# Another hand-written order for the head of a retention and two-GLU kernel

## The chip, the core and the metric

One core of one Trainium2 chip runs the whole program. The metric is device microseconds (us) of one execution, lower is better. The kernel before takes 632.54 us (median of 3 runs, 631.24 to 632.9).

## The reference, cut to what matters

A retention layer (linear attention with a decay for each of 8 heads) over 2 sequences of 768 tokens feeds a GLU (1536 tokens, 512 to 1536 to 512), whose output feeds a normalised SwiGLU of the same size.

```python
for t in range(S):                       # retention; gamma depends on the head
    state = gamma * state + k_t (outer) v_t
    y_t   = scale * q_t @ state
x = y.reshape(1536, 512)
x = ((x @ w_a) * (x @ w_b)) @ w_out      # first GLU
xn = x / sqrt(mean(x * x) + 1e-6) * rms_g
out = (silu(xn @ w_gate) * (xn @ w_val)) @ w_out2
```

## The kernel before, in words

The retention is computed in 12 chunks n = 0 to 11 of 128 tokens; chunk n belongs to sequence n mod 2, so chunk n needs the state that chunk n - 2 left. The GLUs work in f32r with every operand split into a high and a low part (three TensorE passes for a product). Weights come from HBM as 64-bit numbers and are converted on ScalarE and VectorE.

Nothing is scheduled at run time: each engine and each DMA queue executes its instructions in the order in which the Python code issues them, and an instruction whose operand is not ready holds up all behind it on its engine. For the head, that is the retention and the first four products of the first GLU, this order is the string HEAD: a list of tokens, a letter and a number, each looked up in the table `does` and called in turn. After the head a planner places the rest of the two GLUs; its clocks are set equal when the head is over.

What the tokens issue, with their engine:

- `lw`, `lq`, `lk`, `L`, `m`, `d`: loads by the SP queue. `lw` is the next weight tile (`raw`), `lq n` the q and k of the scores of chunk n, `lk n` its k and v, `L n` both, `m` the mask, `d` the query decay `dq_sb` (256 KB; all the others 512 KB). The tiles of `lq` have three buffers, so a fourth load of this kind waits until the scores have read the first.
- `warm n`: n TensorE products of a tile of zeros, whose result is not used.
- `S n` (`scores`): 8 TensorE products q times k into two banks `sc`, then two VectorE products with the mask, `p` (one for each bank).
- `W n`, `w n` (`prep_v`): v times its decay, `vd`, on VectorE or on GpSimd. `Q n`, `q n` (`prep_q`): q times its decay, `qd`, on GpSimd or on VectorE. `D c`: the decay of a later pair of chunks on ScalarE.
- `T n` (`state`): 8 TensorE products `vd` times k into the state `st`, all states in one bank, then a ScalarE copy of it, `sd`, for chunk n + 2. The next T waits for that copy.
- `P n` (`past`): 8 TensorE products of `sd` and `qd` (nothing for chunks 0 and 1). `V n` (`values`): 8 TensorE products of `p` and v into the same banks `ya`; ScalarE rounds them to `xh`, VectorE makes the rest `xl`. `F n`: a ScalarE copy `xf`.
- `c`, `x`: `c` begins the conversion of the next weight tile, `x` issues the next step of each conversion under way (ScalarE `u` and `v`; VectorE a shift, a bit merge, an addition; ScalarE `uh`; VectorE `ul`).
- `Ua i`, `Ub i` (`half`): the two halves, 12 TensorE products of 512 columns each, of product i of the first GLU. `G`, `R`: gate and split of its result. `t`: a step of the tasks that follow.

The lines of the profile name the helper that issues (L87 for VectorE, ScalarE and GpSimd, L96 for TensorE), so work is told apart by its tiles.

Of the kernel before, what the change touches and what calls it, by code (L numbers as in the profile page):

```python
# [11 lines left out]
AF = mybir.ActivationFunctionType  # L12
# [3 lines left out]
B, H, S, D = 2, 8, 768, 64  # L16
P = 128
# [23 lines left out]


FIRST = (0, 0), (0, 1), (1, 0), (1, 1)
HEAD = "lw lq0 m lk0 L1 lq2 d warm15 c0 lk2 x x S0 lq3 lw lk3 warm5 W0 x x P0 V0 F0 x w1 Q2 x T0 S1 L4 lw lw P1 T1 V1 F1 S2 P2 V2 S3 F2 Q3 w2 c0 x W3 P3 x V3 F3 T2 x D2 S4 x L5 L6 Q4 W4 Ua0 L7 T3 x c1 x Q5 W5 x Ub0 G0 x R0 S5 T4 P4 V4 F4 x L8 D3 Q6 W6 x S6 T5 P5 V5 F5 c1 L9 Q7 W7 x S7 x T6 P6 V6 x L10 D4 F6 W8 x P7 Q8 V7 S8 T7 x L11 F7 q9 W9 x t0 x t1 c1 x Ua1 x Ub1 G1 x S9 T8 P8 V8 x R1 D5 Q10 x t1 c1 x Ua2 x x Ub2 G2 x S10 P9 V9 x Q11 x t1 R2 x T9 Ua3 x x x Ub3 G3 x S11 T10 P10 V10 x t1 R3 P11 V11"
UP = {"P1": (1, 0), "P2": (5, 1), "P6": (4, 2), "P7": (3, 3), "P5": (2, 4), "P3": (7, 5), "P4": (6, 6)}


# [20 lines left out]
def retention_glu_swiglu(ctx: ExitStack, tc: tile.TileContext, qk, kv, dq, mask, dg, eye, w1, w2, rg, out):  # L68
# [22 lines left out]
    vec, act, gps = Engine(nc.vector, "vec", 70, 1.04), Engine(nc.scalar, "act", 100, 0.83), Engine(nc.gpsimd, "gps", 120, 2.2)  # L91
# [12 lines left out]
    def mult(o, a, b, engine=vec):  # L104
        engine.tensor_tensor(o, a, b, op=ALU.mult)
# [9 lines left out]
    scale = cst.tile([P, LINE // 4], F32R, name="scale")[:, :2 * NB * TPB].rearrange("p (w j t) -> p w j t", j=NB, t=TPB)  # L115
# [9 lines left out]
    def bank(tag, name):  # L125
        if tag in rings:
            rings[tag].append(rings[tag].pop(0))
            tag = rings[tag][-1]
        return ps.tile([P, TB], F32, tag=tag, name=name)
# [11 lines left out]
    def load_w():  # L141
        if n_load[0] < len(kinds):
            f, s = kinds[n_load[0]]
            t = cp.tile([P, DM, 2], I32, tag="raw", bufs=3, name=f"raw{f}_{s}")
            src = (w1 if f < NF else w2)[f % NF, :, s, :].bitcast(I32)
            nc.sync.dma_start(t.rearrange("p n t -> p (n t)"), src)
            raws[f, s] = t
            n_load[0] += 1
# [94 lines left out]
    class Task:  # L243
# [3 lines left out]
        def step(self):  # L247

            was, after_pe[0], ends[0] = after_pe[0], self.ready, 0.0
            got = next(self.g, "done")  # L250
            after_pe[0] = was
            self.ready = max(self.ready, ends[0])
            if got == "done":
                tasks.remove(self)
            elif got in work:
                self.on = got
            return got != "wait"
# [94 lines left out]
    def rest(ffn, f, j, h, engine=vec):  # L352
        hh, hl = hs[ffn, f, j]
        sub(hl, h, hh.bitcast(F32), engine=engine)
        h_ready.add((ffn, f, j))
# [206 lines left out]
    with tc.manual_schedule():  # L562

        xf = {}
        with ExitStack() as att:
# [7 lines left out]
            dk_sb = dg_sb[:, :CPB * H].rearrange("p (c h) -> p c h", h=H)  # L573
            gq_sb = dg_sb[:, CPB * H:CPB * (H + NP)].rearrange("p (c n) -> p c n", n=NP)
            st = bank("S", "st").rearrange("p (b n d) -> p b n d", b=B, n=NP)
            qk_t, kv_t = {}, {}
# [13 lines left out]
            qd_t, vd_t, sd_t, p_t, ya_t, y_t, dq_t = {}, {}, {}, {}, {}, {}, {1: dq_sb}  # L590
# [6 lines left out]
            def prep_q(n, engine=gps):  # L597
                if n >= B:
                    qd_t[n] = ap.tile([P, NP, C], F32, tag="qd", bufs=QD, name=f"qd{n}")
                    mult(qd_t[n], qk_t[n][:, 0], dq_t[n // B], engine=engine)  # L600

            def prep_v(n, engine=vec):
                c = n // B
                if c < CPB - 1:
                    vd_t[n] = ap.tile([P, H, D], F32, tag="vd", name=f"vd{n}")
                    mult(vd_t[n], kv_t[n][:, 1], dk_sb[:, c, :, None].to_broadcast([P, H, D]), engine=engine)

            def scores(n):
                p_t[n] = a2.tile([P, 2, NP, C], F32, tag="p", name=f"p{n}")
# [76 lines left out]
            def half(i, r):  # L686
                f, j = FIRST[i]
                if r == 0:
                    g_t[i] = one.tile([P, TB], F32, tag=f"g{n_unit[0] % 2}", name=f"g{n_unit[0]}")
                    n_unit[0] += 1  # L690
                b = bank("A", f"c{f}_{j}_{r}")
                passes = [(2 * k + e, w[:, o, e * P:(e + 1) * P], x) for k, o in enumerate(((1, 5), (0, 6))[r]) for e in range(2)
                          for w, x in zip((ups[f][0], ups[f][0], ups[f][1]), (xs[0, j][y] for y in (0, 1, 0)))]
                if f == r == 0:
                    passes.sort(key=lambda p: p[2] is xs[0, j][1])
                for n, (k, w, x) in enumerate(passes):
                    mm(b, w, x[:, k, :], start=(n == 0), stop=(n == len(passes) - 1))
                if r == 0:
                    act.copy(g_t[i], b)
                else:  # L700
                    g_t[i, 1] = b
                    jobs(0, f, j)
# [8 lines left out]
            w = bank("A", "w")[:, :P]  # L711
# [7 lines left out]
            def sums(n):  # L719
# [3 lines left out]
                else:  # L723
                    task(G - EARLY["t"], prep_t(0, xf[0], xf[1]))

            does = {"q": lambda n: prep_q(n, vec), "S": scores, "T": state, "P": past, "V": values, "F": keep, "D": prep_dq, "Q": prep_q, "W": prep_v, "w": lambda n: prep_v(n, gps), "L": load,
                    "lq": load_q, "lk": load_k, "lw": lambda n: load_w(), "c": start_conv, "x": lambda n: step(), "warm": keep_warm,
                    "m": lambda n: nc.sync.dma_start(mask_sb.rearrange("p r n c -> p (r n c)"), mask), "d": lambda n: nc.sync.dma_start(dq_sb, dq),
                    "Ua": lambda i: half(i, 0), "Ub": lambda i: half(i, 1), "G": gated, "R": lambda i: rest(0, *FIRST[i], g_t[i]), "t": sums}
            for o in HEAD.split():  # L730
                name = o.rstrip("0123456789")
# [33 lines left out]
        for ffn in range(2):  # L765
# [9 lines left out]
            for f in range(G, NF):  # L775
# [8 lines left out]
                for o in order.split():  # L784
# [8 lines left out]
                    if o[0] in "bB" and o[1] == "2":  # L793
                        n = f - (o[0] == "B")
# [58 lines left out]
```

## Time and profile before

| | us |
|---|---|
| median of 3 runs | 632.54 |
| lowest and highest | 631.24, 632.9 |
| profiled execution | 634.35 |
| its span, first to last instruction | 632.6 |
| TensorE busy in the span | 620.4 |
| VectorE busy | 508.1 |
| ScalarE busy | 313.3 |
| GpSimd busy | 15.0 |

The profiled execution took 1.8 us more than the median, and 1.8 us of it lie outside the span. Engines are called PE (TensorE), DVE (VectorE), ACT (ScalarE), POOL (GpSimd) and SP (the queue that issues the loads) in the rows. A TensorE product in plain f32 appears as two records, so eight products are x16. Times in a timeline count from the first instruction.

### The profile page before, as it was taken

How to read it: one execution, taken by the hardware profiler on the slowest of the kernel's cores; microseconds unless marked ns; L12 is line 12 of the kernel's file. 1: busy time of each engine (PE TensorE's matmuls, PEld its weight loads, DVE VectorE, ACT ScalarE, POOL GpSimd, SP SyncE). 2: the span in 40 equal slices, each digit the busy share in tenths (PEclk: the TensorE clock that was granted, in tenths of full speed). 3: DMA queues.
4: the chain of work that ended last, by engine and by line, in shares of the span. 5: the costliest groups of instructions: out<-in, count | busy, mean ns of one | idle time of the engine just before them, and what ended most of it. 6: DMA issues, size and time to landing. Idle time of an engine off the chain costs nothing.

```text
span 632.6 us, 8559 instructions
## 1 busy us (share of the span) xinstructions
PE 620.4 (98%) x3264; PEld 510.2 (81%) x3264; DVE 508.1 (80%) x881; ACT 313.3 (50%) x600; POOL 15.0 (2%) x16
## 2 busy tenths in 40 slices
PE   7999999999999999999999999999999999999997
PEld 7777888888888888888877887888888888888886
DVE  4679798798988988788778898698888978788554
ACT  3456365663545454444444768574464464373230
POOL 1221100000000000000000000000000000000000
PEclk9889999999999999999999999999999999999999
DMA  9857122122322222123300022223222321220004
GB/s 343 308 190 282 34 67 67 42 94 66 101 68 66 74 93 71 61 70 99 101 0 2 0 72 92 71 68 99 67 66 68 100 67 66 67 67 1 0 18 183
DMA packets 16456, 54.91 MB, mean 87 GB/s; under 512 B 2080, under 2 KB 2464, under 8 KB 16416
## 3 DMA queue, kind: packets, MB, share of 16 engines
q1 hardware_dynamic: 16128, 54.21, 26.3%
q8 instruction: 25, 0.41, 0.3%
q10 hardware_dynamic: 288, 0.17, 0.1%
q14 instruction: 15, 0.12, 0.1%
HBM read 51.22 MB, written 3.15 MB: 86 GB/s over the span
## 4 chain that ended last, share of the span: by engine, by line
PE 88%; DVE 8%; ACT 3%; issue 1%; DVEq 0%; ACTq 0%
PE b L96 29%; PE y L96 27%; PE c L96 26%; PE ya L96 2%; DVE u L87 2%; DVE acc L87 1%; PE sc L96 1%; DVE p L87 1%; PE w L96 1%; DVE xl L87 1%; DVE ul L87 1%; ACT uh L87 1%; ACT sq L87 1%; DVE vd L87 1%; DVE sq L87 0%
## 5 line engine op out<-in xcount | busy, mean ns | idle before, releaser
L87 DVE TENSOR_TENSOR acc<-y,acc 128x512 f32<-128x512 f32 (+1 forms) x121 | 82.2, 682 | 26.7 <-PE y L96 25.7
L96 PE MATMUL c<-xh,uh 128*128 128x512 f32 x256 | 101.1, 395 | 1.0 <-ACT uh L87 1.0
L96 PE MATMUL c<-xh,ul 128*128 128x512 f32 x256 | 100.5, 393 | 0.5 <-DVE ul L87 0.5
L96 PE MATMUL c<-xl,uh 128*128 128x512 f32 x256 | 99.2, 391 | 0.0
L87 DVE TENSOR_TENSOR ul<-wt,uh 128x512 fp32r<-128x512 f32 (+1 forms) x122 | 60.8, 511 | 18.3 <-ACT uh L87 17.8
L96 PE MATMUL b<-xh,uh 128*128 128x512 f32 x160 | 62.4, 390 | 0.1
L96 PE MATMUL b<-xl,uh 128*128 128x512 f32 x160 | 62.3, 389 | 0.0
L96 PE MATMUL b<-xh,ul 128*128 128x512 f32 x160 | 62.3, 389 | 0.0
L96 PEld LDWEIGHTS c<-xh,uh 128*128 128x128 f32 x256 | 48.5, 189 | 11.4 <-ACT uh L87 1.2
L96 PE MATMUL y<-hh,oh 128*128 128x512 f32 x144 | 56.4, 392 | 1.1 <-DVE acc L87 1.1
L96 PEld LDWEIGHTS c<-xh,ul 128*128 128x128 f32 x256 | 48.4, 189 | 11.0 <-DVE ul L87 0.9
L96 PE MATMUL y<-oh,hh 128*128 128x512 f32 x144 | 56.3, 391 | 0.3 <-ACT acc L87 0.3
L96 PEld LDWEIGHTS c<-xl,uh 128*128 128x128 f32 x256 | 48.5, 190 | 9.9
L96 PE MATMUL y<-hl,oh 128*128 128x512 f32 x144 | 56.2, 390 | 0.1
L96 PE MATMUL y<-ol,hh 128*128 128x512 f32 x144 | 56.2, 390 | 0.0
L96 PE MATMUL y<-hh,ol 128*128 128x512 f32 x144 | 56.1, 389 | 0.0
L96 PE MATMUL y<-oh,hl 128*128 128x512 f32 x144 | 56.0, 389 | 0.0
L87 ACT CAST uh<-wt 128x512 fp32r<-128x512 f32 (+1 forms) x122 | 53.3, 478 | 0.8 <-DVE wt L87 0.7
L87 DVE TENSOR_TENSOR t<-t,b 128x512 f32<-128x512 f32 x60 | 41.0, 683 | 14.9 <-ACT t L87 8.5
L87 ACT COPY t<-b 128x512 f32<-128x512 f32 x40 | 23.5, 587 | 57.7 <-PE b L96 57.3
L87 ACT ACTIVATE v<-raw 128x512 int32<-128x512 uint32 x72 | 47.9, 665 | 0.0
L96 PE MATMUL b<-th,uh 128*128 128x512 f32 x120 | 46.9, 391 | 0.0
(98 smaller groups left out, 1114.7 us busy)
## 6 DMA issues: line engine op xcount, KB each, us to landing
raw<-in_w SPq DMA_DIRECT2D x72, 512.0 KB, 3.5
q<-in_qk SPq DMA_DIRECT2D x12, 512.0 KB, 5.6
k<-in_kv SPq DMA_DIRECT2D x12, 512.0 KB, 6.6
out<-acc SPq DMA_DIRECT2D x11, 256.0 KB, 2.0
mask_sb<-in_mask SPq DMA_DIRECT2D x1, 512.0 KB, 5.8
dq_sb<-in_dq SPq DMA_DIRECT2D x1, 256.0 KB, 8.2
out<-acc SPq DMA_DIRECT2D x1, 128.0 KB, 1.7
out<-acc ACTq DMA_DIRECT2D x1, 128.0 KB, 1.8
```

What stands on the lines that cost most here:

```text
L87: return getattr(self.engine, op)(out, *a, **k)
L96: nc.tensor.matmul(out, *a, **k)
```

## The change

HEAD is written anew. Of its differences these matter below: 13 warming products before `S0` and not 15; `d` is issued before the loads of chunk 1, and `lq3` before `lq2`; `S1` stands before `T0`, and `V1` before `T1`; the steps of the first weight conversion are spread later; `T3` and `T4` stand around the first half product `Ua0`. Chunk 7's `vd` goes from VectorE to GpSimd (`W7` to `w7`), and the `qd` of chunks 10 and 11 from GpSimd to VectorE (`Q10`, `Q11` to `q10`, `q11`). A form of `prep_v` on ScalarE is added, token `v`, which HEAD does not use. From the end of the head on, every engine's order is the same in both kernels.

```diff
-HEAD = "lw lq0 m lk0 L1 lq2 d warm15 c0 lk2 x x S0 lq3 lw lk3 warm5 W0 x x P0 V0 F0 x w1 Q2 x T0 S1 L4 lw lw P1 T1 V1 F1 S2 P2 V2 S3 F2 Q3 w2 c0 x W3 P3 x V3 F3 T2 x D2 S4 x L5 L6 Q4 W4 Ua0 L7 T3 x c1 x Q5 W5 x Ub0 G0
...
+HEAD = "lw lq0 m lk0 d L1 lq3 lq2 lk2 warm13 x c0 x x S0 lw lk3 warm5 x W0 P0 V0 F0 x w1 S1 Q2 L4 x T0 lw lw P1 V1 F1 T1 S2 P2 V2 F2 Q3 w2 c0 S3 x T2 W3 P3 x x V3 F3 x S4 x T3 L5 L6 D2 Q4 W4 L7 c1 Ua0 x Q5 W5 T4 x Ub0
...
@@ prep_v @@
-                    mult(vd_t[n], kv_t[n][:, 1], dk_sb[:, c, :, None].to_broadcast([P, H, D]), engine=engine)
+                    if engine is act:
+                        for h in range(H):
+                            act.activation(vd_t[n][:, h], kv_t[n][:, 1, h], AF.Copy, scale=dk_sb[:, c, h:h + 1])
+                    else:
+                        mult(vd_t[n], kv_t[n][:, 1], dk_sb[:, c, :, None].to_broadcast([P, H, D]), engine=engine)
...
+ "v": lambda n: prep_v(n, act)
```

TensorE around the scores of chunk 1, before. Tile `sc1` holds these scores, `st` the state, `ya1` the values of chunk 1; the numbers at the end are the buffers'.

```order
L96 MATMUL ya0_1_157<-p0_127,k0_97 64x128
L96 MATMUL st_86<-vd0_151,k0_97 64x64 x8
L96 MATMUL sc1_0_194<-q1_99 128x128
...
L96 MATMUL st_86<-vd1_178,k1_101 64x64 x8
L96 MATMUL ya1_0_214<-p1_193,k1_101 64x128
```

The same place after:

```order
L96 MATMUL ya0_1_154<-p0_127,k0_97 64x128
L96 MATMUL sc1_0_176<-q1_100 128x128
...
L96 MATMUL st_86<-vd0_151,k0_97 64x64 x8
L96 MATMUL ya1_0_211<-p1_175,k1_102 64x128
...
L96 MATMUL st_86<-vd1_173,k1_102 64x64 x8
```

The scores of chunk 1 have moved ahead of the first state, and the second state behind the values of chunk 1.

VectorE from the first scores to the masked scores `p1`, before (`ISA` is the addition that ends the conversion of `u0_0`, `ul0` the low part that follows from it):

```order
L87 TENSOR_TENSOR vd0_151<-k0_97,dg_sb_85 128x512
L87 TENSOR_SCALAR u0_0_123<-u0_0_123 128x512
L87 SCALAR_TENSOR_TENSOR u0_0_123<-raw0_0_92,u0_0_123 128x512
L87 ISA u0_0_123<-u0_0_123,v0_0_124 128x1024
L87 TENSOR_TENSOR xl0_0_159<-ya0_0_156,xh0_0_158 128x2x128
L87 TENSOR_TENSOR xl0_0_159<-ya0_1_157,xh0_0_158 128x2x128
L87 TENSOR_TENSOR ul0_176<-u0_0_123,uh0_175 128x2x256
L87 TENSOR_TENSOR p1_193<-sc1_0_194,mask_sb_84 128x512
```

And after, down to the place where `ul0` now stands:

```order
L87 TENSOR_SCALAR u0_0_123<-u0_0_123 128x512
L87 SCALAR_TENSOR_TENSOR u0_0_123<-raw0_0_92,u0_0_123 128x512
L87 TENSOR_TENSOR vd0_151<-k0_97,dg_sb_85 128x512
L87 TENSOR_TENSOR xl0_0_156<-ya0_0_153,xh0_0_155 128x2x128
L87 TENSOR_TENSOR xl0_0_156<-ya0_1_154,xh0_0_155 128x2x128
L87 ISA u0_0_123<-u0_0_123,v0_0_124 128x1024
L87 TENSOR_TENSOR p1_175<-sc1_0_176,mask_sb_84 128x512
...
L87 TENSOR_TENSOR p3_278<-sc3_1_280,mask_sb_84 128x512
L87 TENSOR_TENSOR ul0_195<-u0_0_123,uh0_194 128x2x256
```

`ul0` has moved from ahead of `p1` to behind `p3`.

The SP queue, the loads of chunks 1 to 3, before:

```order
L580 DMA q1_99<-in_qk 128x1024
L584 DMA k1_101<-in_kv 128x1024
L580 DMA q2_103<-in_qk 128x1024
L728 DMA dq_sb_83<-in_dq 128x512
L584 DMA k2_121<-in_kv 128x1024
L580 DMA q3_140<-in_qk 128x1024
L146 DMA raw0_1_142<-in_w1 128x1024
```

And after:

```order
L732 DMA dq_sb_83<-in_dq 128x512
L580 DMA q1_100<-in_qk 128x1024
L584 DMA k1_102<-in_kv 128x1024
L580 DMA q3_104<-in_qk 128x1024
L580 DMA q2_106<-in_qk 128x1024
L584 DMA k2_108<-in_kv 128x1024
L146 DMA raw0_1_140<-in_w1 128x1024
```

The query decay has moved ahead of chunk 1, and q3 ahead of q2, so that it is now q2 that takes the buffer of q0.

## Rows read from the trace of the kernel before

**Rows 1.** Page, part 1: busy time of each engine, share of the span, instructions.
```profile
PE 620.4 (98%) x3264; PEld 510.2 (81%) x3264; DVE 508.1 (80%) x881; ACT 313.3 (50%) x600; POOL 15.0 (2%) x16
```
**Rows 2.** Windows: stretch, length, busy PE, PEld, DVE, ACT, POOL; PEclk, DMA, GB/s.
```profile
7.10:37.60 30.50, 25.32 (x276) 20.09 (x275) 18.94 (x30) 11.72 (x31) 8.04 (x6) 0.89 0.86 328
37.60:51.50 13.90, 13.73 (x257) 11.37 (x256) 13.28 (x23) 9.86 (x29) 3.78 (x3) 1.00 0.60 217
...
150.00:600.00 450.00, 447.88 (x1988) 368.34 (x1988) 375.94 (x662) 230.57 (x425) 0.00 (x0) 1.00 0.21 62
```
**Rows 3.** Windows: the stretches around two falls of the granted clock.
```profile
13.10:16.50 3.40, 1.25 (x20) 0.91 (x22) 2.63 (x3) 1.19 (x4) 1.27 (x1) 1.00 1.02 402
16.50:19.90 3.40, 3.40 (x30) 3.07 (x29) 0.76 (x2) 1.35 (x4) 2.26 (x2) 0.50 1.03 411
...
30.20:33.60 3.40, 1.90 (x22) 0.97 (x20) 3.40 (x4) 2.60 (x5) 2.11 (x2) 1.00 0.51 188
33.60:37.00 3.40, 3.40 (x8) 2.70 (x9) 0.46 (x1) 0.00 (x0) 0.00 (x0) 0.50 0.74 274
```
**Rows 4.** Timeline, PE: start, length, work, [idle before]: S to V; S, T, P, V; halves.
```profile
22.54 1.16 PE L96 MATMUL sc<-q 64*128 64x128 f32 x16
...
25.07 0.98 PE L96 MATMUL ya<-p,k 128*64 128x128 f32 x13 [0.17 <-DVE p L87]
...
40.93 1.16 PE L96 MATMUL sc<-q 64*128 64x128 f32 x16
42.02 0.69 PE L96 MATMUL st<-vd,k 128*64 128x64 f32 x16
42.63 0.67 PE L96 MATMUL ya<-qd,sd 64*64 64x128 f32 x16
43.23 1.09 PE L96 MATMUL ya<-p,k 128*64 128x128 f32 x16
44.26 1.16 PE L96 MATMUL sc<-q 64*128 64x128 f32 x16
...
51.54 0.50 PE L96 MATMUL c<-xh,uh 128*128 128x512 f32 x1
...
57.23 1.16 PE L96 MATMUL sc<-q 64*128 64x128 f32 x16
```
**Rows 5.** Timeline, PE: the warming products, first and second group.
```profile
1.05 6.09 PE L96 MATMUL w<-warm 128*128 128x128 f32 x30 [1.05 <-DVE warm L87]
...
8.17 1.38 PE L96 MATMUL w<-warm 128*128 128x128 f32 x10
```
**Rows 6.** Timeline, all engines, 13 to 18 us.
```profile
13.29 1.27 POOL L87 TENSOR_TENSOR qd<-q,dq_sb 128x512 f32<-128x512 f32 x1 [0.34 <-DMA dq_sb<-in_dq]
...
13.68 1.43 DVE L87 TENSOR_TENSOR ul<-u,uh 128x512 fp32r<-128x512 f32 x1 [0.96 <-ACT uh L87]
14.02 0.69 PE L96 MATMUL st<-vd,k 128*64 128x64 f32 x16 [1.76 <-issue]
...
15.03 1.28 DVE L87 TENSOR_TENSOR p<-sc,mask_sb 128x512 f32<-128x512 f32 x2
...
16.36 1.85 PE L96 MATMUL ya<-p,k 128*64 128x128 f32 x14 [0.17 <-DVE p L87]
...
18.15 2.00 PE L96 MATMUL sc<-q 64*128 64x128 f32 x16
```
**Rows 7.** Timeline, PE: the first product of the half Ub0.
```profile
32.33 0.50 PE L96 MATMUL c<-xh,uh 128*128 128x512 f32 x1 [1.05 <-ACT uh L87]
```
**Rows 8.** Timeline, SP and POOL: the load of q0; GpSimd products that waited for loads.
```profile
1.16 0.42 SPq L580 DMA_DIRECT2D q<-in_qk  x1
...
11.41 1.54 POOL L87 TENSOR_TENSOR vd<-k,dg_sb 128x512 f32<-128x512 f32 x1 [10.58 <-DMA k<-in_kv]
...
17.01 1.26 POOL L87 TENSOR_TENSOR qd<-q,dq_sb 128x512 f32<-128x512 f32 x1 [2.44 <-DMA q<-in_qk]
```
**Rows 9.** DMA issues at 1.16 us; the last figure is us to landing.
```profile
q<-in_qk SPq DMA_DIRECT2D x1, 512.0 KB, 5.0
```

More of the change, by code (lines that the diff above doesn't have):

```diff
@@ L43 @@
 FIRST = (0, 0), (0, 1), (1, 0), (1, 1)
-HEAD = "lw lq0 m lk0 L1 lq2 d warm15 c0 lk2 x x S0 lq3 lw lk3 warm5 W0 x x P0 V0 F0 x w1 Q2 x T0 S1 L4 lw lw P1 T1 V1 F1 S2 P2 V2 S3 F2 Q3 w2 c0 x W3 P3 x V3 F3 T2 x D2 S4 x L5 L6 Q4 W4 Ua0 L7 T3 x c1 x Q5 W5 x Ub0 G0 x R0 S5 T4 P4 V4 F4 x L8 D3 Q6 W6 x S6 T5 P5 V5 F5 c1 L9 Q7 W7 x S7 x T6 P6 V6 x L10 D4 F6 W8 x P7 Q8 V7 S8 T7 x L11 F7 q9 W9 x t0 x t1 c1 x Ua1 x Ub1 G1 x S9 T8 P8 V8 x R1 D5 Q10 x t1 c1 x Ua2 x x Ub2 G2 x S10 P9 V9 x Q11 x t1 R2 x T9 Ua3 x x x Ub3 G3 x S11 T10 P10 V10 x t1 R3 P11 V11"
+HEAD = "lw lq0 m lk0 d L1 lq3 lq2 lk2 warm13 x c0 x x S0 lw lk3 warm5 x W0 P0 V0 F0 x w1 S1 Q2 L4 x T0 lw lw P1 V1 F1 T1 S2 P2 V2 F2 Q3 w2 c0 S3 x T2 W3 P3 x x V3 F3 x S4 x T3 L5 L6 D2 Q4 W4 L7 c1 Ua0 x Q5 W5 T4 x Ub0 x D3 G0 S5 P4 V4 R0 F4 x L8 Q6 W6 x S6 T5 P5 V5 F5 c1 x L9 Q7 w7 x T6 S7 P6 V6 F6 x L10 D4 Q8 W8 P7 T7 V7 F7 S8 x x L11 q9 W9 x t0 t1 c1 x x Ua1 Ub1 G1 x x S9 P8 R1 x D5 T8 q10 V8 x t1 c1 Ua2 x x Ub2 x G2 x R2 S10 P9 V9 x q11 t1 T9 x Ua3 x x Ub3 G3 S11 x R3 T10 P10 P11 V10 x x t1 V11"
 UP = {"P1": (1, 0), "P2": (5, 1), "P6": (4, 2), "P7": (3, 3), "P5": (2, 4), "P3": (7, 5), "P4": (6, 6)}
@@ L724, in sums @@
                     task(G - EARLY["t"], prep_t(0, xf[0], xf[1]))
-            does = {"q": lambda n: prep_q(n, vec), "S": scores, "T": state, "P": past, "V": values, "F": keep, "D": prep_dq, "Q": prep_q, "W": prep_v, "w": lambda n: prep_v(n, gps), "L": load,
+            does = {"q": lambda n: prep_q(n, vec), "S": scores, "T": state, "P": past, "V": values, "F": keep, "D": prep_dq, "Q": prep_q, "W": prep_v, "w": lambda n: prep_v(n, gps), "v": lambda n: prep_v(n, act), "L": load,
                     "lq": load_q, "lk": load_k, "lw": lambda n: load_w(), "c": start_conv, "x": lambda n: step(), "warm": keep_warm,
```

## The prediction

> **What bounds the kernel now.** I read the page's busy times first: TensorE is busy 620.4 of 632.6 us, VectorE 508.1 [rows 1]. The reader is to see that a change elsewhere pays only where TensorE stands still or runs slowly. The windows say where: from 150 to 600 us TensorE is busy 447.88 of 450.00, and from 37.60 to 51.50, in the head, 13.73 of 13.90. From 7.10 to 37.60 it is busy 25.32 of 30.50, at a mean granted clock of 0.89 [rows 2]. All there is to win lies there.
>
> Busy time understates it, since a record is long when the clock is low. So I count that stretch in steps that ran without a wait, from start to next start [rows 4]: S 42.02 - 40.93 = 1.09, T 0.61, P 0.60, V 1.03, and a half product (57.23 - 51.54)/2 = 2.85. Between S0 (7.1, as the warming products end, [rows 5]) and S5 (37.60) the kernel before does five S, four V, four T, two P, two halves and five warming products (1.31, just under the 1.38 of their rows): 5.45 + 4.12 + 2.44 + 1.20 + 5.70 + 1.31 = 20.2 us of work in 30.5. **10.3 us are lost.** Where:
>
> - T1 waits 1.76 until 14.02. V1's second part starts only at 16.36, since `p1` starts at 15.03: VectorE stood first in `ul0`, 1.43 us beside a GpSimd product of 1.27 [rows 6].
> - That idle stretch, 1.25 busy of 3.40, is followed by 3.40 us at half clock (0.50, the 1.2 GHz level), so that V1's rest and S2 take 16.36 to 18.15 and 2.00 instead of 1.16 [rows 3, 6]. The same again at 33.60, after 1.90 busy of 3.40: there Ub0 had waited 1.05 for `uh` [rows 3, 7]. Two falls at half rate are worth up to 2 x 1.70.
> - The rest is the wait in each chunk between S and V: from the start of S3 (22.54) to the second part of V3 (25.07) pass 2.53 us [rows 4], which S and P fill to 1.69.
>
> **The change, part by part, as a walk along TensorE.** I take times of the profiled execution and carry the difference to the median (632.54; the profiled execution took 634.35).
>
> *Two warming products fewer.* 30 records take 6.09 us, 0.20 each; a later group of 10 takes 1.38, 0.14 each [rows 5]. So these products began at the lower clock; the last ones ran at the upper, by the second group's rate, where two products (4 records) cost 0.55; from the whole group's mean 0.81. Records overlap at their ends, so the step is a little shorter than these: I take 0.45 to 0.5, S0 at 6.6. q0 does not forbid it: issued at 1.16, landed 5.0 later, at 6.2 [rows 8, 9].
>
> *The loads.* The DMA engines are saturated at 402 to 411 GB/s [rows 3], so 512 KB take 1.28 us and the order alone says what lands when. Before, k1 had landed by 11.4, the decay by 13.3, q3 by 17.0 [rows 6, 8]. With the decay (256 KB, 0.64) ahead, q1 lands at 11.4 - 1.28 + 0.64 = 10.7, k1 at 12.0, q3 at 13.3. q2 now waits for S0 to free its buffer, with k2 and the next weight tile behind it on SP; S0 ends at 7.8, while three to four loads are still queued (to 13.3), so the DMA engines don't run dry: cost nothing as long as S0 ends before about 12. q2 lands at 14.6, k2 in q3's old place, 17.0. Later loads keep their places.
>
> *S1 ahead of T0, V1 ahead of T1, `ul0` behind `p3`.* V0 ends at 10.1 (8.17 + 1.31 - 0.45 + 1.03); S1 waits for q1 until 10.8, a new wait of 0.7; T0 follows, 11.9 to 12.5. `p1` no longer stands behind `ul0`; by the 2.53 of chunk 3, V1's second part starts at 10.8 + 2.53 = 13.3 and ends at 14.3 (before: 18.15). What VectorE must do before `p1` (two shifts and merges, `vd0`, `xl0`, the addition) is some six products at 0.6 (half of `p`'s 1.28 for two, [rows 6]) after `p0` at 9.1: about 12.3, just covered by S1. T1 has its `vd1` (12.0 + 1.54 = 13.6) and runs 14.3 to 14.9.
>
> *S2 to S4.* S2 at 14.9 (q2 14.6), **3.2 us earlier** than 18.15. V2's second part at 14.9 + 2.53 = 17.4, k2 is there at 17.0; end 18.5. S3 18.5, T2 and P3 in the gap (until 20.8), V3's second part 21.0, end 22.1. S4 to 23.2, T3 to 23.8.
>
> *The half products.* Ua0 to 26.6, T4 to 27.2, Ub0 to 30.1, and 0.2 for the handover (Ua0's and Ub0's waits included): S5 at 30.3. VectorE's last duties here are `ul0` (first), `vd3`, shift and merge, `xl`, the addition, `p4`, `vd4` and the second `ul0`: ten products of 0.6 after `p3` at 21.0 is 27.0. That is the tightest spot: it covers T4 (26.6, needs `vd4` at 26.5) with 0.1 to spare, and if VectorE is later, T4 and Ub0 are later by as much. No GpSimd product runs beside it (its next needs the decay `dq2`, behind that conversion on ScalarE).
>
> Before, S5 began at 37.60 and T4 was still to come (0.6). So the head stands 37.6 + 0.6 - 30.3 = **7.9 us earlier**, of which 0.45 are warming, 1.76 + 1.7 the waits of T1 and V1 (16.36 - 14.63), about 3.3 the two falls of the clock, the rest Ub0's wait and T's and P's put into gaps, less 0.7 + 0.4 of new waits for loads.
>
> *The three products on the other engine.* `vd7` leaves VectorE (0.61), `qd10` and `qd11` come to it (1.22); none stands on TensorE's path while VectorE is in time. A product beside GpSimd's can take 1.43 where 0.68 is usual (1.28 for two), so each pairing costs up to 0.75 [rows 6]; there is one GpSimd product fewer. Bounds: +0.6 + 0.75 of VectorE time and -1.5, on TensorE's path between 0 and +1.3; I take 0, since GpSimd is busy only 3.78 of the 13.90 us there [rows 2] and TensorE still ran 13.73. The Trainium skill, page SBUF — State Buffer, section Who interferes with whom, says that a VectorE instruction with two SBUF inputs and a GpSimd instruction that reads SBUF shut each other out for a whole instruction; the trace agrees for `ul0` (1.43). By it `vd7` on GpSimd could block VectorE for its full 1.27, and the gain would be some 0.5 smaller at most, an estimate from that row.
>
> *Behind S5* TensorE has no idle time to lose or win [rows 2], all engines' order after the head is unchanged, so the shift stays: 632.5 - 7.9 = 624.6.
>
> **The rivals.**
>
> *The clock falls once more (626.2).* The new waits lie at 10.1 to 10.8 and 12.5 to 13.3, with V1's first part between: some 1.4 us idle between 10.1 and 13.4, less than in either stretch that a fall followed (1.5 and more of 3.40) [rows 3]. Half clock then slows V1, T1, S2: up to 3.40/2 = 1.7, less what waiting for q2 and k2 absorbs. For it: fewer warming products. Against: the stretches before the two falls were emptier.
>
> *VectorE takes over (628.5).* From 37.60 to 51.50 it is busy 13.28 of 13.90 [rows 2]. If TensorE starts this stretch 7.9 early and VectorE only half of it, because of the spot at 26.5 and four or five pairings with GpSimd at 0.75, about 4 us are given back. Against: VectorE idles 30.50 - 18.94 = 11.6 us before 37.60, and it shifts along.
>
> *Slower: the clock is not granted in the head (636).* If, with 13 products, the higher clock comes only when Ua0 runs (or is lost at once in S0 to T3), the 14.2 us of S, T, P, V and warming work between 6.6 and 23.8 take 28.4, from 6.6 to 35.0: 11.2 later than in the walk, net +3.3. It decides beyond some 8 us of half-rate work. Against: with fifteen products the rate rose while they were still running [rows 5], and the 13 end only 0.45 earlier. The Trainium skill, page TensorE: Matmul & The Clock Gate, section What's actually happening, calls the throttled state the default, which activity releases; that agrees with the slow first products, and by it fewer products are a risk.
>
> *The shift is eaten later (632).* Were the stretch after the head set by weight loads and conversions, an early head would only wait. Against: 447.88 of 450 busy [rows 2].
>
> **How the numbers follow.** Forecast 624.6, own range 623 to 626: 0.58. Clock falls once, 626.2: 0.18. VectorE, 628.5: 0.12. More gained than walked (S-to-V waits shorter, 622): 0.04. Eaten later: 0.03. Slower: 0.05. A measurement of this kernel can tell 0.3%, 1.9 us, from no change; faster than 630.6 are the first four, 0.92; same 0.03; slower 0.05. The range is 622 to 628.5; it leaves out the last two and the far half of VectorE's case.
>
> **What would show it.** Right: S1 near 10.8 behind a wait for a load, `p1` near 12.1, S2 near 15, no 0.50 in the clock between 13 and 37, S5 near 30, Ua1 near 43 instead of 51.54, the rest unchanged. Wrong: a stretch at 0.50 between 10 and 20; T4 or Ub0 waiting for `vd` or `ul`; TensorE waiting for VectorE between 30 and 60; idle TensorE after 60.

## The result, and the profile after

| | before | after |
|---|---|---|
| median, us | 632.56 (4 runs, 631.24 to 632.9) | 625.24 (4 runs, 625.16 to 625.47) |
| ratio, 95% interval | | 0.9889 [0.9872, 0.9906] |
| profiled execution, us | 634.35 | 625.31 |
| its span | 632.6 | 623.5 |

The changed kernel is 7.3 us faster; 624.6 was forecast, 0.6 less than was measured. The medians differ by 7.3 us, the two profiled executions by 9.0. That second number matters below: executions of the kernel before differ from one another by up to 4.6 us within one group of runs, those of the changed kernel by 0.3.

Busy time on the page of the changed kernel (the row that answers to [rows 1]):

```profile
PE 614.6 (99%) x3260; PEld 505.9 (81%) x3260; DVE 505.1 (81%) x882; ACT 313.7 (50%) x600; POOL 13.1 (2%) x15
```

TensorE's busy time fell by 5.8 us although only four records are gone: a record is long at half clock (S2 took 2.00 in [rows 6], 1.16 after). The same windows as in [rows 2, 3] (stretch, length, busy PE, PEld, DVE, ACT, POOL, then granted clock, DMA share, GB/s):

```profile
7.10:37.60 30.50, 28.78 (x422) 23.46 (x420) 24.93 (x44) 17.04 (x46) 11.14 (x9) 1.00 0.96 374
37.60:51.50 13.90, 13.72 (x189) 11.18 (x187) 12.61 (x23) 8.99 (x24) 1.66 (x2) 1.00 0.74 280
150.00:600.00 450.00, 447.91 (x1988) 368.28 (x1987) 374.27 (x658) 230.71 (x422) 0.00 (x0) 1.00 0.21 63
13.10:16.50 3.40, 3.27 (x62) 2.81 (x62) 1.43 (x4) 1.63 (x5) 1.96 (x3) 1.00 1.02 402
```

The head is where it changed: 422 records lie between 7.10 and 37.60 where 276 lay, TensorE is busy 28.78 of 30.50, and no stretch has a clock of 0.50 any more. From 150 to 600 us nothing moved. TensorE's timeline of the changed kernel, with the steps that answer to [rows 4, 6, 7]: S0, S1, T0, the second part of V1, T1, S2, V2, T4, S5, Ua1 (start, length, work, idle before):

```profile
6.17 1.16 PE L96 MATMUL sc<-q 64*128 64x128 f32 x16 [0.28 <-DMA q<-in_qk]
...
10.69 1.16 PE L96 MATMUL sc<-q 64*128 64x128 f32 x16 [0.75 <-DMA q<-in_qk]
11.78 0.69 PE L96 MATMUL st<-vd,k 128*64 128x64 f32 x16
...
13.22 0.98 PE L96 MATMUL ya<-p,k 128*64 128x128 f32 x13 [0.17 <-DVE p L87]
...
14.04 0.73 PE L96 MATMUL st<-vd,k 128*64 128x64 f32 x15
14.71 1.16 PE L96 MATMUL sc<-q 64*128 64x128 f32 x16
...
16.95 1.38 PE L96 MATMUL ya<-p,k 128*64 128x128 f32 x16 [0.41 <-DMA k<-in_kv]
...
26.48 0.69 PE L96 MATMUL st<-vd,k 128*64 128x64 f32 x16
...
30.04 1.16 PE L96 MATMUL sc<-q 64*128 64x128 f32 x16
...
42.96 0.50 PE L96 MATMUL c<-xh,uh 128*128 128x512 f32 x1 [0.18 <-ACT xh L87]
```

And the masked scores `p1` on VectorE, 15.03 in [rows 6]:

```profile
11.88 1.29 DVE L87 TENSOR_TENSOR p<-sc,mask_sb 128x512 f32<-128x512 f32 x2
```

The walk holds: every step from S0 to S5 stands within 0.45 us of where it was forecast, S5 at 30.04 for 30.3, and the only waits left are those for q1 (0.75), q0 and k2 and handovers of a few tenths. The question for the experiments is therefore not where the kernel gained, but what each part of the gain is, and why the sum of the profiles and the sum of the medians are not the same.

### The profile page after: what moved, and what is told of

Same layout as the page of the kernel before. It is cut to its first block, busy times and chain, and to the rows that moved or that the text cites. A ratio compares the mean times of both kernels' runs of the same rounds, so it can differ in the third digit from the quotient of the medians.

```text
span 623.5 us, 8550 instructions
## 1 busy us (share of the span) xinstructions
PE 614.6 (99%) x3260; PEld 505.9 (81%) x3260; DVE 505.1 (81%) x882; ACT 313.7 (50%) x600; POOL 13.1 (2%) x15
## 4 chain that ended last, share of the span: by engine, by line
PE 89%; DVE 5%; ACT 3%; DMA 2%; issue 1%; SPq 0%; DVEq 0%; ACTq 0%
PE b L96 29%; PE y L96 28%; PE c L96 27%; PE ya L96 2%; DMA k<-in_kv 1%; DVE acc L87 1%; PE sc L96 1%; DVE u L87 1%; DMA q<-in_qk 1%; PE st L96 1%; DVE xl L87 1%; ACT sq L87 1%; ACT uh L87 0%; DVE sq L87 0%; PE rb L96 0%
## 5 line engine op out<-in xcount | busy, mean ns | idle before, releaser
L87 DVE TENSOR_TENSOR acc<-y,acc 128x512 f32<-128x512 f32 (+1 forms) x121 | 82.3, 682 | 26.6 <-PE y L96 25.6
L87 DVE TENSOR_TENSOR t<-t,b 128x512 f32<-128x512 f32 x60 | 41.0, 683 | 14.9 <-ACT t L87 8.5
```

What stands on the lines that cost most here:

```text
L87: return getattr(self.engine, op)(out, *a, **k)
```

## The experiments

The kernels of one group ran on one chip, beside runs of the kernel before there: 26 in the first group (e0 to e3), 9 in the second (e4, e6, e7, e9), 13 in the third (e11, e5, e8, e10).

**e0: the kernel before once more.** No edit.

> The kernel before once more, for its clock. The profiled execution of before lost up to 3.4 us to two falls of the clock and took 1.8 us more than the median. Theory A (the clock's falls differ from execution to execution): some executions of this kernel hold one fall and take about 631 to 632.6, others two and take about 634; the span and the mean clock move together. Theory B (the falls are the same in all executions, and the 1.8 us lie elsewhere): every execution has a mean clock of 0.993 and the times differ without it.

Median 632.33 us (10 runs, 630.3 to 634.72), ratio 1.0 [0.9978, 1.0023]. Windows of this profile, then T1 and V1 in it:

```profile
12.05:15.45 3.40, 1.23 (x22) 0.77 (x18) 2.44 (x6) 1.86 (x5) 2.52 (x2) 1.00 1.04 405
15.45:18.86 3.41, 3.25 (x27) 2.90 (x28) 0.89 (x3) 1.00 (x4) 0.87 (x2) 0.50 1.02 407
29.80:33.20 3.40, 1.90 (x21) 1.28 (x21) 3.40 (x4) 2.61 (x5) 1.67 (x1) 1.00 0.69 242
```
```profile
14.03 0.69 PE L96 MATMUL st<-vd,k 128*64 128x64 f32 x16 [1.84 <-ACT sd L87]
...
15.63 1.97 PE L96 MATMUL ya<-p,k 128*64 128x128 f32 x14 [0.16 <-DVE p L87]
```

The same kernel, with the same gap ahead of T1 (1.23 busy of 3.40) and the same gap ahead of Ub0 (1.90 of 3.40, just as in [rows 3]), has one fall of the clock here and two in the profile before. Over 58 executions of the kernel before (26, 9 and 13 beside the groups, 10 as e0) the times go with the mean granted clock: four at 0.999 took 630.28 to 630.48, 38 at 0.996 or 0.997 took 631.14 to 633.33, 16 at 0.993 to 0.995 took 632.15 to 634.85. The profile at 0.997 has one fall, that of [rows 3], at 0.993, two. If the mean clock counts the falls, as these two profiles suggest, executions with one take 0.7 to 2.9 us more than those without, most executions have one, and the profiled one of [rows 3] had one more than most.

The mean clock does not explain all of the spread. At 0.996 and 0.997 the times form two groups, 25 at 631.1 to 631.9 and 13 at 632.7 to 633.3. One thing besides the clock that differs can be seen: `ul0` took 1.43 us in [rows 6] and takes 0.69 here, so `p1` starts at 14.30 and not 15.03, and V1's second part starts 1.60 behind T1 and not 2.34. Whether this makes the two groups is not shown. The rows also name what T1 waits for: ScalarE's copy `sd` of the first state, which stands behind `uh` there (13.04 to 13.66).

**e1 and e2: the two halves of the change.** e1 has the new order as far as T1 and the old one from S2 on; e2 the old one as far as V1 and the new one from S2 on.

```diff
 e1, against the changed kernel
-S2 P2 V2 F2 Q3 w2 c0 S3 x T2 ... S4 x T3 L5 L6 D2 Q4 W4 L7 c1 Ua0 x Q5 W5 T4 x Ub0
+S2 P2 V2 S3 F2 Q3 w2 c0 x ... T2 x D2 S4 x L5 L6 Q4 W4 Ua0 L7 T3 x c1 x Q5 W5 x Ub0
...
 e2, against the changed kernel
-lw lq0 m lk0 d L1 lq3 lq2 lk2 warm13 x c0 x x S0 lw lk3
+lw lq0 m lk0 L1 lq2 d warm15 c0 lk2 x x S0 lq3 lw lk3
...
-w1 S1 Q2 L4 x T0 lw lw P1 V1 F1 T1 S2
+w1 Q2 x T0 S1 L4 lw lw P1 T1 V1 F1 S2
```

> The new order up to the state of chunk 1, the old one from the scores of chunk 2 on. Theory of the walk: S2 starts near 14.8 instead of 18.15, and about 3.3 to 4 of the 7.3 us are gained (about 628.5 to 629.2). Rival (the gain lies in the second part, and the first part's is eaten by loads): under 1 us gained, 631.6 or more.

> The old order up to the values of chunk 1, the new one from the scores of chunk 2 on. Theory of the walk: S2 near 18, then the wait before the half product Ub0 and the fall of the clock behind it are gone, T4 stands in the gap: 3.5 to 4.5 us gained (about 628 to 629). Rival (the first part alone gives the gain): about 632.

e1: 628.96 us (10 runs), 0.9952 [0.9936, 0.9968]; eight runs at a clock of 0.999 or more took 628.52 to 629.21, two at 0.996 took 630.3. e2: 628.35 us (8 runs), 0.9938 [0.9918, 0.9959]; one run at 0.999 took 627.15, seven at 0.997 took 628.2 to 629.9. Both medians lie within their forecasts. S2 stands at 14.99 in e1; in e2 it stands at 16.71 and not near 18, since `ul0` takes 0.69 there too. At full clock, where the kernel before takes 630.4, the early half is worth about 1.45 us and the late half about 3.2 (one run). Together 4.7. The median before lies 2.2 above 630.4, put down here to the falls and what comes beside them; the last 0.4 of the 7.3 is within what the groups differ by.

**e3: `ul0` back ahead of `p1`, all else as in the changed kernel.**

```diff
-w1 S1 Q2 L4 x T0 lw lw P1
+w1 x x S1 Q2 L4 T0 lw lw P1
```

> The changed kernel with one step moved back: ul0, the low part of the first converted weights, stands on VectorE ahead of p1 again. Theory (ul0 held p1): p1 starts at about 13.1 to 13.7 instead of 11.9, S2 1.2 to 1.8 us later, 626.5 to 627, and up to 1.7 more if the clock falls behind the new gap. Rival (the order of scores, states and values on TensorE gave it): 625.2 to 625.5.

628.40 us (7 runs, 627.3 to 629.01), 0.9939 [0.9916, 0.9962]: 3.2 us above the changed kernel. VectorE's and then TensorE's timeline, and two windows:

```profile
12.65 1.24 DVE L87 TENSOR_TENSOR ul<-u,uh 128x512 fp32r<-128x512 f32 x1 [0.69 <-ACT uh L87]
13.81 1.27 DVE L87 TENSOR_TENSOR p<-sc,mask_sb 128x512 f32<-128x512 f32 x2
```
```profile
14.54 2.35 PE L96 MATMUL ya<-p,k 128*64 128x128 f32 x15 [1.84 <-DVE p L87]
```
```profile
11.34:14.75 3.41, 1.56 (x32) 1.28 (x28) 2.72 (x5) 1.42 (x4) 1.04 (x1) 1.00 1.05 416
14.75:18.16 3.41, 3.33 (x34) 2.91 (x34) 0.94 (x3) 0.80 (x3) 3.09 (x3) 0.50 1.00 396
```

One VectorE product in the wrong place costs twice. `p1` starts at 13.81 instead of 11.88, V1 waits 1.84, and the clock falls behind the gap. The two runs without a fall took 627.3, 1.6 to 2.1 over the changed kernel; the five with it 628.4 to 629.0, another 1.1 to 1.7.

**e4: only `ul0` moved.** The kernel before, with this one step of the conversion behind `p3`.

```diff
-w1 Q2 x T0 S1 L4 lw lw P1 T1 V1 F1 S2 P2 V2 S3 F2
+w1 Q2 T0 S1 L4 lw lw P1 T1 V1 F1 S2 P2 V2 S3 x F2
```

> The kernel before with one step moved: ul0 behind p3, nothing else. Theory (ul0 held p1, but T1 in front of V1 waits until 14.0 for the copy of the first state and for vd1 in any case): V1's second part starts near 14.8 instead of 15.6 to 16.4, so 0.8 to 1.7 us are gained at equal clock (before without a fall of the clock 630.3 to 630.5, here 628.8 to 629.6); the move pays in full only together with V1 ahead of T1. Rival (ul0 alone is the first part's gain): 3 us, about 627.5 at equal clock.

629.05 us (6 runs), 0.9952 [0.9937, 0.9968]: five runs at a clock of 1.0 took 628.86 to 629.21, one at 0.996 took 630.98, and that is the profiled one. The stretch with T1's wait, and S0, T1 and S2 in e4; then S0, S1 and S2 in e1:

```profile
11.80:15.20 3.40, 1.64 (x40) 1.47 (x37) 2.23 (x5) 1.84 (x5) 2.54 (x2) 1.00 1.04 404
```
```profile
7.19 1.16 PE L96 MATMUL sc<-q 64*128 64x128 f32 x16
...
14.13 0.69 PE L96 MATMUL st<-vd,k 128*64 128x64 f32 x16 [1.76 <-issue]
...
15.62 1.16 PE L96 MATMUL sc<-q 64*128 64x128 f32 x16
```
```profile
6.43 1.16 PE L96 MATMUL sc<-q 64*128 64x128 f32 x16 [0.30 <-DMA q<-in_qk]
...
10.97 1.16 PE L96 MATMUL sc<-q 64*128 64x128 f32 x16 [0.77 <-DMA q<-in_qk]
...
14.99 1.16 PE L96 MATMUL sc<-q 64*128 64x128 f32 x16
```

T1's wait of 1.76 is still there in e4, and yet S2 follows S0 by 8.43 us, in e1 by 8.56. At full clock e4 takes 629.0 and e1 628.9. So one step brings as much as the whole early half of the change: `ul0` no longer holds up `p1`. The forecast time was right; its clause that the move pays in full only with V1 ahead of T1 was not. S1 ahead of T0 and V1 ahead of T1 take away T1's wait and put others in its place: that for q1 (0.77 in e1), and V1's for `p1`, whose second part starts at 13.51 in e1 where T0 ends near 12.7. The clock stays full behind T1's wait in all six runs of e4, though it is 1.76 in one piece and the stretch is nearly as empty as e3's (1.64 busy of 3.40, there 1.56).

**e6: the three products back on their old engines. e7: the loads of chunks 1 to 3 in their old order.** Both are the changed kernel otherwise.

```diff
 e6
-w7 ... q10 ... q11
+W7 ... Q10 ... Q11
 e7
-m lk0 d L1 lq3 lq2 lk2 warm13 x c0 x x S0 lw lk3
+m lk0 L1 lq2 d warm13 x c0 lk2 x x S0 lq3 lw lk3
```

> The changed kernel with the three products back on their old engines (vd of chunk 7 on VectorE, qd of chunks 10 and 11 on GpSimd). Theory (none of them stands on TensorE's path): 625.0 to 625.5, like the changed kernel, and the clock full throughout. Rival (VectorE is the bound from 37 to 60 us): 0.6 to 1.5 us away from 625.2, either way.

> The changed kernel with the loads of chunks 1 to 3 in the old order (q1, k1, q2, decay, k2, q3). Theory (the load order shifts waits but V1 and V2 are set by p1 and p2 on VectorE): S1 starts at 10.0 instead of 10.7, V1's second part still near 13.2, S2 near 14.7, 624.9 to 625.5. Rival (the new load order carries part of the gain): 0.6 to 1.3 us slower.

e6: 625.64 us (4 runs), 0.9895 [0.9874, 0.9917]. e7: 625.75 us (4 runs), 0.9897 [0.9878, 0.9916]. The changed kernel did not run in this group; it took 625.24 in its first runs and 625.75 in the third group, so neither part shows a worth beyond that 0.5. The 0.5 itself is there from the first loads on: q1 lands 7.4 us after its issue in the first profile and 7.9 in e11, S1 starts at 10.69 and 11.21, S5 at 30.04 and 30.54. In e7 (rows of S1 and V1) q1 is there earlier, and V1 waits for `p1` in its stead, so that S2 starts at 14.93:

```profile
10.38 1.16 PE L96 MATMUL sc<-q 64*128 64x128 f32 x16
...
12.85 0.43 PE L96 MATMUL ya<-p,k 128*64 128x128 f32 x2 [0.69 <-DVE p L87]
```

**e11 and e5: the changed kernel, and it with fifteen warming products.**

```diff
-warm13
+warm15
```

> The changed kernel unchanged, as the yardstick of this group. Expected 625.2 to 625.8 in every execution, granted clock 0.999 or 1.0, no fall in the head: S0 between 6.2 and 6.8, S1 near 10.7, S2 near 14.9, S5 near 30.2. Rival (the clock falls in the changed kernel too, only more rarely): some executions 1.2 to 2.5 us longer at 0.997.

> The changed kernel with the fifteen warming products of the kernel before. Theory (S0 came at 6.17 because q0 landed at 6.13, so the step of two warming products is cut short by the load; S1 then waits 0.75 for q1 anyway, which absorbs up to that much): S0 0.3 to 0.5 later, S1 not later, total within 0.2 us of the changed kernel, 625.2 to 625.8. The prediction's sum (warming products shift everything behind them): 0.45 longer, 625.7 to 626.2. Rival (fewer warming products cost or save a fall of the clock): more than 1 us of difference, with another granted clock.

e11: 625.75 us (4 runs, 625.57 to 625.9), 0.9892 [0.987, 0.9913], granted clock 1.0 in all. e5: 625.94 us (4 runs, 625.69 to 626.04), 0.9894 [0.9872, 0.9916]. Two products more are 0.2 us by the medians, and the ranges overlap. S0 comes at 7.12 in e5 and 6.89 in e11, S1 at 11.13 and 11.21, S2 at 15.28 and 15.22: S1 waits for q1 in both (0.38, 0.63), which swallows the difference. The theory named q0 as what limits S0; that was so in the profile after (q0 landed at 6.1), not in e11, where S0 starts as the warming products end. How long this group takes differs more from run to run than two products are worth: the same 26 records took 4.83 in the first profile of the changed kernel and 5.91 in e11.

**e8: the gap ahead of T1 filled with seven products of zeros, in the kernel before.** Nothing waits less for it.

```diff
-T0 S1 L4
+T0 S1 warm7 L4
```

> The kernel before with seven warming products between S1 and T1, into TensorE's wait for the first conversion, so that this stretch is no longer idle and nothing else moves. Theory (the idle stretch ahead of T1 is what brings the first fall of the clock, the wait ahead of Ub0 the second): no execution has the first fall any more; executions without a fall 630.3 to 630.8, those with the second one 631.3 to 633.3, none with two (above 633.5); if the trace has a 0.50 it lies at 30 to 37 us. Rival (the falls come by themselves, whatever TensorE did): as the kernel before, most executions with one fall and some with two, median 631.5 to 632.5, a 0.50 between 14 and 20 us in the trace or times above 633.5.

630.27 us (10 runs), 0.9963 [0.9951, 0.9975]; granted clock 0.999 or 1.0 in all ten, nine of them within 629.95 to 630.43. The tenth took 631.53 at a clock of 1.0. Windows, and from S0 on TensorE's timeline of e8:

```profile
12.05:15.45 3.40, 2.88 (x34) 2.37 (x34) 2.34 (x5) 1.86 (x5) 2.46 (x2) 1.00 1.04 405
15.45:18.86 3.41, 3.16 (x48) 2.38 (x48) 1.93 (x4) 1.35 (x4) 1.33 (x2) 1.00 1.03 410
28.70:32.10 3.40, 1.90 (x9) 1.28 (x8) 2.79 (x3) 2.03 (x5) 1.03 (x1) 1.00 0.89 300
32.10:35.50 3.40, 3.40 (x51) 2.69 (x53) 1.92 (x4) 0.80 (x2) 0.00 (x0) 1.00 0.52 182
```
```profile
6.85 1.16 PE L96 MATMUL sc<-q 64*128 64x128 f32 x16
...
11.96 1.83 PE L96 MATMUL w<-warm 128*128 128x128 f32 x14
13.79 0.69 PE L96 MATMUL st<-vd,k 128*64 128x64 f32 x16
...
16.42 1.16 PE L96 MATMUL sc<-q 64*128 64x128 f32 x16
...
29.76 0.50 PE L96 MATMUL c<-xh,uh 128*128 128x512 f32 x1 [1.05 <-ACT uh L87]
...
30.94 0.51 PE L96 MATMUL c<-xh,ul 128*128 128x512 f32 x1 [0.45 <-DVE ul L87]
...
33.44 1.16 PE L96 MATMUL sc<-q 64*128 64x128 f32 x16
...
75.23 0.50 PE L96 MATMUL y<-hh,oh 128*128 128x512 f32 x1
```

Useless work in a wait makes the kernel 2.4 us faster (632.69 to 630.27 in this group), down to the time of the four executions without a fall (630.28 to 630.48). So 2.4 is what the falls, with what comes beside them, cost the median of this group; against 630.4 it is 1.2 in the first group (median 631.64) and 1.4 in the second (631.79). The tenth run of e8 shows that 1.2 us can come without a fall. The theory is right on the first fall and too careful on the second: that one is gone as well, though Ub0 still waits 1.05 and 0.45 and its stretch is as empty as before (1.90 of 3.40). In e4, which has the same waits there, one run of six has that fall, so none in ten may still be chance:

```profile
27.00:30.40 3.40, 1.92 (x21) 1.11 (x20) 3.40 (x4) 2.60 (x5) 1.94 (x2) 1.00 0.90 314
30.41:33.83 3.42, 3.42 (x9) 2.65 (x9) 0.28 (x1) 0.00 (x0) 0.00 (x0) 0.50 0.75 274
```

e8 and e11 make a clean pair: same chip, full clock, S0 at 6.85 and 6.89. S0, S2, S5 and the first product `y` behind the head in e11:

```profile
6.89 1.22 PE L96 MATMUL sc<-q 64*128 64x128 f32 x16
...
15.22 1.16 PE L96 MATMUL sc<-q 64*128 64x128 f32 x16
...
30.54 1.16 PE L96 MATMUL sc<-q 64*128 64x128 f32 x16
...
70.89 0.50 PE L96 MATMUL y<-hh,oh 128*128 128x512 f32 x1
```

| stretch on TensorE | e8 | e11 | gain |
|---|---|---|---|
| S0 to S2 | 9.57 | 8.33 | 1.24 |
| S2 to S5, T4 included | 17.63 | 15.32 | 2.31 |
| S5 to Ua1 (47.39 and 43.46), T4 not included | 13.34 | 12.92 | 0.42 |
| Ua1 to the first `y` | 27.84 | 27.43 | 0.41 |

Where T4 stands on the other side of S5, its 0.61 is added or taken off. The gains sum to 4.4, the spans of the two profiles differ by 4.4, and the medians by 4.5. Of the 2.31, Ub0's two waits are 1.50, and T2 between S3 and P3 another 0.47 (S3 to S4 takes 4.02 in e8, 3.55 in e11).

**e9 and e10: an own order with earlier loads.** The first weight tile is loaded behind k2 and converted later, nine warming products suffice; e10 has chunk 2's `vd` ahead of chunk 3's `qd` on GpSimd as well.

```diff
 e9
-lw lq0 m lk0 d L1 lq3 lq2 lk2 warm13 x c0 x x S0 lw lk3 warm5 x W0 P0 V0 F0 x w1
+lq0 m lk0 L1 lq2 d lk2 lw warm9 S0 lq3 lk3 warm5 W0 P0 V0 F0 w1
 e10, against e9
-F2 Q3 w2 S3
+F2 w2 Q3 S3
```

> A further order, to test that what is left between 6 and 22 us is set by the arrival of loads: the first weight tile is loaded behind k2 and not first, the conversion's steps move behind the scores of chunks 2 to 4, and 9 warming products stand before S0. Theory (loads bound): q0 lands near 4.9, q1 near 8.7 instead of 10.7, S2 near 13 instead of 14.7, S5 near 28.5 instead of 30.0, 623.5 to 624. Rival 1 (VectorE or the conversions then bind, Ua0 or Ub0 wait): 625. Rival 2 (fewer products and emptier gaps make the clock rise late or fall): 625 to 626.5.

> The changed kernel with the first weight tile loaded behind k2 and the first conversion later, nine warming products, and chunk 2's vd ahead of chunk 3's qd on GpSimd, so that the state of chunk 2 no longer stands behind a load it doesn't need. Theory (the 1.9 us which the earlier loads brought to S2 were lost at T2, because GpSimd works in order): T2's wait of 1.55 is gone, S4 and T4 come 1 to 1.5 earlier, and the total is 624.2 to 624.9. Rival (the head is bound by the whole of loads and VectorE work, and the time goes to another wait): T2 is earlier but S4, T4 or S5 wait for a load or for uh instead, total 625.2 to 626.

e9: 625.84 us (4 runs), 0.9898 [0.9879, 0.9917]. The theory's 623.5 to 624 did not come. S2 stands at 12.83, 1.9 us earlier than in the changed kernel's first profile, and at T2 it is given back. GpSimd and TensorE in e9:

```profile
17.12 1.82 POOL L87 TENSOR_TENSOR qd<-q,dq_sb 128x512 f32<-128x512 f32 x1 [4.05 <-DMA q<-in_qk]
...
18.91 1.03 POOL L87 TENSOR_TENSOR vd<-k,dg_sb 128x512 f32<-128x512 f32 x1
...
20.00 0.69 PE L96 MATMUL st<-vd,k 128*64 128x64 f32 x16 [1.55 <-POOL vd L87]
```

GpSimd took them in order: `qd` waited 4.05 for q3, and `vd`, whose k2 was there (in e10 it starts at 13.03), stood behind it. e10 takes that wait away, and its rival wins: 625.57 us (4 runs, 625.45 to 625.61), 0.9889 [0.9863, 0.9914], where e11 took 625.57 to 625.9. S3 and T4 in e10:

```profile
17.08 1.25 PE L96 MATMUL sc<-q 64*128 64x128 f32 x16 [0.97 <-DMA q<-in_qk]
...
26.53 0.69 PE L96 MATMUL st<-vd,k 128*64 128x64 f32 x16 [0.84 <-ACT uh L87]
```

T2 no longer waits, S4 comes 1.3 earlier than in e9 (20.92 for 22.23), and then the state of chunk 4 stands at 26.53, within 0.05 of the changed kernel's 26.48, behind the conversion of the second weight tile. The row names `uh`; T4 itself reads `vd4`, which VectorE makes behind that conversion's addition, from 25.74 to 26.42. So in e10 the head from Ua0 on is set by the conversion, not by when the chunks began. No version tried is faster than the changed kernel by more than 0.2 us.

## Why the prediction was right, and where it was not

**The place and the walk: right.** The loss was looked for between S0 and S5, and all but 0.8 us of the gain lies there. S1 at 10.69 behind a wait of 0.75 (10.8 and 0.7 forecast), `p1` at 11.88 (12.1), S2 at 14.71 (14.9), V2's wait for k2 0.41 (0.4), T4 at 26.48 (26.6), S5 at 30.04 (30.3), Ua1 at 42.96 (43). None of the signs named under "Wrong" appeared.

**The terms of the sum: three were too large, two too small.** By the walk the head stands 7.9 earlier. The runs of the third group give:

| term | forecast | measured |
|---|---|---|
| two warming products | 0.45 | 0 to 0.2 (e5) |
| waits of T1 and V1, less the new wait for q1 | 1.76 + 1.7 - 0.7 = 2.8 | 1.2 (S0 to S2) |
| falls of the clock | 3.3 | 2.4 (e8) |
| Ub0's wait, T's and P's in gaps ("the rest"), less the new wait for k2 | 1.8 - 0.4 = 1.4 | 2.3 (S2 to S5) |
| behind S5 | 0 | 0.8 |
| sum | 7.9 | 6.7 to 6.9 (the third group's medians differ by 6.9) |

- *"I carry the difference to the median."* This step failed. The profiled execution had two falls and took 1.8 us more than the median, as the prediction notes; the median execution has one fall. The term of 3.3 belonged to that one execution. What falls cost the median, with what comes beside them, is 2.4 by e8 and less in the other groups. The two profiles differ by 9.0, so carried from profile to profile the 7.9 is 1.1 too small, and the two misses cancel in part.
- *T1 and V1.* The prediction counted T1's wait (1.76) and V1's (1.7) and took only the waits for loads off. V1's 1.7 holds 0.7 of that one execution again, `ul0` at 1.43: in e0, where it took 0.69, V1's wait is 1.0 (T1 ends at 14.64, V1's second part starts at 15.63). And T1's wait gives less than its length: the walk itself has V1 waiting from 12.5 to 13.3, some 0.8 which the sum leaves out. By e4, with `ul0` out of the way, T1 waits its full 1.76 and S2 follows S0 as closely as in e1. The cause that counts is `p1`, which the prediction names.
- *Behind S5 nothing.* "No idle time to lose or win" was read from a busy share of 13.73 in 13.90, but the kernel before does more steps there than it must wait for: T7 between P7 and V7 covers the wait for `p7` (P7 to Ua1 less T7 takes 3.35 in e8, 2.82 in e11; 0.1 of it goes to a wait of T6), and P10 next to P11, V10 next to V11 save handovers (S11 to the first `y` takes 4.33 in e8, 4.02 in e11). Busy time can't show what a closer order of the same products is worth.
- *Costs set to nothing.* For the order of the loads (e7) and for the three products (e6) this was right within the 0.5 by which the changed kernel's own medians differ.

The errors cancel: 0.6 us between forecast and result is less than some of them, so the closeness of the total is partly luck; that of the walk is not.

**The rivals.** *The clock falls once more:* no run of the changed kernel shows it. A fall behind waits in this place does occur: e3, with an idle stretch of 1.84 us in one piece, has it in five runs of seven. But e4, with 1.76 in one piece, has none there in six, so the wait alone does not say whether the clock falls. *VectorE takes over:* `vd4`, for which T4 waits, runs from 25.39 to 26.07, where the prediction had it end at 26.5, and T4 follows Ua0 without a wait. *Slower, eaten later:* nothing in the traces; S5 at 30.04 and Ua1 at 42.96 exclude both.

## What to carry to other kernels

Before an order is changed for the sake of an engine that waits, look for the one instruction ahead of its releaser on the releasing engine: a single VectorE step moved out of the way brought as much as the whole new order of the first two chunks, and what is moved earlier only helps until the next load or conversion that is itself late. A profile is one execution: where its granted clock has a stretch at 0.50, take the times of several executions with their mean clock, and count a fall by how many of them have it. Price a wait from more than one profile too: V1's was 1.7 in one and 1.0 in the next. To see what a suspected fall costs, put useless products into the gap in front of it and change nothing else.

## What the runs showed of the hardware

**The same kernel has more or fewer falls of the clock from run to run.** By the mean clock, if it counts the falls, the kernel before had none in 4 of 58 executions, one in 38 and more in 16; the changed kernel, e5, e6, e7, e9 and e10 had none in 28. The stretch at 0.50 begins at 15.45 in e0 and at 14.75 in e3, at 16.50 in [rows 3]. The Trainium skill, page TensorE: Matmul & The Clock Gate, section What's actually happening, says that the gate's observation runs freely, so that a kernel sees more or fewer slow products at its start from run to run; the runs here agree (26 warming records took 4.83 and 5.91) and show a like variation for gaps in the middle of a kernel. Why the gap ahead of Ub0 brings a fall in some runs of the kernel before and in one of e4, and in none of ten of e8 with the same 1.90 busy of 3.40, is open. It may be chance, or what stands 15 us ahead of the gap, in which e8 and e4 differ.

**Which of two engines is held up depends on which began.** In [rows 6] `qd` on GpSimd starts at 13.29 and takes 1.27, `ul0` on VectorE at 13.68 and takes 1.43. In e2 the order of the starts is the other way round:

```profile
13.41 0.69 DVE L87 TENSOR_TENSOR ul<-u,uh 128x512 fp32r<-128x512 f32 x1 [0.96 <-ACT uh L87]
13.63 1.60 POOL L87 TENSOR_TENSOR qd<-q,dq_sb 128x512 f32<-128x512 f32 x1 [0.84 <-DMA dq_sb<-in_dq]
```

Here `ul0` takes its usual 0.69 and `qd` 1.60. The Trainium skill, page SBUF — State Buffer, section Who interferes with whom, says that the order of issue, not the shape of the operation, decides who is blocked; these two rows agree. The 0.7 us of `ul0` counted in [rows 6] only because `p1` stood behind it; in e0, e2 and e8 `ul0` takes 0.69 in the same place, so the prediction's 1.7 for V1 was too large by it.
